# A two-layer kernel behind a retention: the state sums become one scan per unit, weight splits keep out of a block's last two steps, and three casts and splits of the second layer move

## The chip, the cores and the metric

One core of a Trainium2 chip runs the kernel. PE is TensorE (PEld its weight loads), DVE VectorE, ACT ScalarE, POOL GpSimd, SP the engine that issues the DMAs. Every engine takes its own instructions in the order in which the program gives them, and waits where data is missing. The time of a run is device microseconds from start to end of the program; the span of a profile is from the first to the last instruction.

## The reference

```python
def _attn_ref(q, k, v):                    # (4, 8, 576, 64) each
    scores = scale * np.matmul(q, k.transpose(0, 1, 3, 2))
    gamma = 1.0 - 2.0 ** (-5.0 - np.arange(H))
    Dmat = np.where(rel >= 0, gamma[:, None, None] ** rel[None, :, :], 0.0)   # rel = i - j
    return np.matmul(scores * Dmat[None], v)
def _moe_ref(x, w_in, w_out):              # x (2304, 512), w_in (512, 2048), w_out (2048, 512)
    h = x @ w_in
    return (h * (1.0 / (1.0 + np.exp(-1.702 * h)))) @ w_out
def _moe2_ref(x, w_in, w_out, g_ln):       # w_in (512, 1024), w_out (1024, 512)
    h = x @ w_in
    e = np.exp(h - h.max(-1, keepdims=True))
    solu = h * (e / (e.sum(-1, keepdims=True) + 1e-9))
    ln = (solu - mean(solu)) / np.sqrt(var(solu) + 1e-6) * g_ln
    return ln @ w_out
def reference(...):                        # heads side by side make x; then the two layers
    return _moe2_ref(_moe_ref(attn(q, k, v).transpose(0, 1, 3, 2)...))
```

The weights are float64 in memory; everything is computed to about float32.

## The kernel before, in words

**The retention (0 to about 81 us of the profile).** 16 units, one for each pair of heads of one batch, all 128 partitions (64 rows a head). A unit's 576 positions are four chunks of 128 and one of 64. Within a chunk scores are masked by a triangle; what earlier chunks give is carried in a state of 64x64 for each head. PE makes the scores (`st2`, L326), the four chunk states (`states`, L290) and the outputs (`st4`: L347 from the masked scores, L359 and L365 from the states, which are its stationary operand). ACT scales v (`st0`, L278) and copies the states to SBUF (L296). DVE masks (L330), sums the states over the chunks (`st1`, L306: three instructions, each of which needs the one ahead of it) and writes the outputs to `xb` (L377, L382). On DVE and ACT the sequence of a unit is: masks, a piece of weight conversion, outputs of the unit before, state sums. Units are loaded by SP, five buffers in a ring; the constants in two loads.

**The first layer (to about 495 us)** goes over generations `GENS` of the 16 weight slices: slices 0 to 3, 4 to 7, 8 to 15. In each the 2304 tokens go by in six blocks of 384. A step is one slice of one block: `emit_h` (12 matmuls, L417, then the sigmoid L421 on ACT and L422, L426, L427 on DVE) and, one step later, `emit_y` (12 matmuls, L444). Every operand is two numbers, a rounded high part and a low part, and a product is three matmuls: high by high, low by high (of the weight), high by low (of the token tile). The high parts are casts on ACT (L226 of a weight, L398 of a token tile `xs`), the low parts subtractions on POOL (L231, two halves of a weight; L399). `split_x` makes the four token tiles of the next block: tiles 0 and 1 in the block's last step but one, 2 and 3 in its last.

**The background queue** `self.bg` is a list of small pieces: three DVE instructions for each half weight turn float64 words into float32 (`convert`, L203, L206, L209), then come the cast and the two subtractions of `split_weight`, and loads. `background(n)` takes n pieces with a DVE cost and all free ones behind them; `run` calls it at fixed places of each unit and step. So the order on each engine is set by where these calls stand and by what is at the head of the list then. In the first eight slices the two subtractions of a weight are put between the conversions of the next one; the converted weight stands in one of three buffers `T_START`.

**The second layer (to the end)** takes pairs of token tiles; its first product is seven block products instead of eight (`emit_h2`, L520, with weight combinations t1 to t4, b11, b21, b22 and token combinations s1 to s4, a11, a12, a22 from `split_y`; L484 to L489 are sums on DVE). `norm` has three steps: maximum and Exp; product, statistics and a power on POOL (L566); scale (L568). `turn` transposes (L579), `emit_out` makes the second product (L606) with weights w16 to w19. Of these w16 is split along with t3 in the first layer's last block, the casts of w17 to w19 stand at its end, and their subtractions behind the first pair's maximum.

Of the kernel before, what the change touches and what calls it, by code (L numbers as in the profile page):

```python
# [23 lines left out]
P = 128  # L24
# [21 lines left out]
for _name, _w in (  # L46
    ("half", 1), ("g_ln", FB), ("vdec", NP * 3), ("step", NP), ("tri2", LAST), ("tri", CH), ("qdec", NP * CH),
    ("space", 48),
):
    _CC[_name] = (_n, _n + _w)  # L50
    _n += _w
CCONST = _n


def constants():

    gamma = (1.0 - 2.0 ** (-5.0 - np.arange(H))).astype(np.float64)
    c = np.zeros((P, CCONST), np.float64)

    def put(name, a):  # L60
        lo, hi = _CC[name]
        c[:, lo:hi] = a.reshape(P, hi - lo)

    head_of_row = np.arange(P) // D
    qdec = np.zeros((P, NP, CH))
    step = np.zeros((P, NP))
    vdec = np.zeros((P, NP, 3))
    j = np.arange(P)
    for p in range(NP):
        g = gamma[2 * p + head_of_row]  # L70
        qdec[:, p] = g[:, None] ** j[None, :]
        step[:, p] = g ** CH
        for a in range(2):
            vdec[:, p, a] = gamma[2 * p + a] ** -j
        vdec[:, p, 2] = g ** -(j % D)
    put("qdec", qdec)
    put("step", step)
    put("vdec", vdec / math.sqrt(D))
    put("tri", (j[:, None] <= np.arange(CH)[None, :]).astype(np.float64))
    put("tri2", (j[:, None] % D <= np.arange(LAST)[None, :]).astype(np.float64))  # L80
    put("half", np.full((P, 1), -0.5))
    return c.astype(np.float32)
# [54 lines left out]
class Build:  # L137
# [39 lines left out]

    def const(self, name):
        lo, hi = _CC[name]
        return self.at(_M["c"] + lo, hi - lo)  # L180
# [56 lines left out]
    def background(self, n):  # L237

        while self.bg and (n > 0 or not self.bg[0][0]):
            dve, piece = self.bg.pop(0)  # L240
# [4 lines left out]
    def un(self, u):  # L245

        t = self.at(IN_AT[u % NU], CATT)
        st = self.at(ST_AT + (u % 2) * NCH * D, NCH * D).rearrange("r (c e) -> r c e", c=NCH)
# [52 lines left out]
    def st1(self, u):  # L301

        st = self.un(u)[1]
        g = self.const("step")[:, u % NP:u % NP + 1]
        for c in range(1, NCH):
            self.nc.vector.scalar_tensor_tensor(st[:, c], st[:, c - 1], g, st[:, c], ALU.mult, ALU.add)  # L306
# [308 lines left out]
    def run(self):  # L615
# [33 lines left out]
        others = []  # L649
        for f in range(FH):  # L650
            t = T_START[f % 3]
# [3 lines left out]
            for n, p in enumerate(pieces):  # L655
                self.bg.append((1, p))
                if others and n in (0, 4):
                    self.bg.append((0, others.pop(0)))
            hi, *others = self.split_weight(f, t)
            self.bg.append((0, hi))  # L660
        self.bg += [(0, p) for p in others]
# [40 lines left out]
        for g, j, f in steps:  # L702
# [7 lines left out]
            if g == 1 and j == 0 and fl == 1:  # L710

                for i in range(4):
                    first, *rest = self.split_weight(FH + i, T_LATER[i])
                    self.bg += [(1, first)] + [(0, p) for p in rest]
# [9 lines left out]
            bg = 1  # L724
            if fl:
                self.background(bg)
# [3 lines left out]
            if prev is not None:  # L730
                self.emit_y(*prev)
                pg, pj, pf = prev
                if pj == NB - 1:
# [3 lines left out]
                    elif pg == 2:  # L737
# [4 lines left out]
                        if b == "t3":  # L742
                            held += self.split_weight(NF, T_LATER[4], (self.ysp, 2))
# [3 lines left out]
            self.background(1 + (0 if fl else bg))  # L747
# [21 lines left out]
        def out(t):  # L769
# [3 lines left out]
        last = [self.split_weight(NF + i, T_LATER[4 + i], pool) for i, pool in (  # L773
            (1, (self.ysp, 2)), (2, None), (3, (self.zsp, 1))
        )]
        for p in last:
            p[0]()
        y1 = self.split_y(1)
        for piece in y1[:3]:
            piece()  # L780
# [7 lines left out]
        self.emit_h2(0, {"p3": lambda: run(y1[3:])})  # L788
        self.norm(0, 1)
        self.norm(1, 1)  # L790
        for p in last:
            run(p[1:])
# [7 lines left out]
        self.emit_h2(1, {"u2": lambda: self.norm(0, 2, 3), "p3": start})  # L800
# [104 lines left out]
```

## Time and profile before

| | |
|---|---|
| median of 3 runs | 712.52 us (709.82 to 713.21) |
| the profiled execution | 712.1 us, of which the span is 710.3 us |
| PE busy | 685.2 us (96%) |
| DVE busy | 513.4 us (72%) |
| ACT, POOL busy | 231.3 us, 222.8 us |

Matmuls are pipelined and their ends are modelled, so 96% does not mean PE at its peak; how far it is bound has to be read stretch by stretch. A name such as h<-xs,w tells output and inputs of an instruction.

### The profile page before, as it was taken

The numbers are of one execution on the slowest core, as the hardware profiler recorded it, in microseconds if no ns is written. First come the engines' busy times: TensorE is split into PE (matmuls) and PEld (weight loads), VectorE is DVE, ScalarE is ACT, GpSimd is POOL, SyncE is SP. The second block draws the span as 40 slices with busy tenths as digits, with TensorE's granted clock in tenths as the row PEclk, the third lists the DMA queues.
The fourth block names the chain that finished last, engine by engine and source line by source line (L and its number), as shares of the span: only waits on it lengthen the run. The fifth ranks groups of instructions, "written<-read, shape, count | busy, mean of one in ns | idle before, by whom it ended". The sixth has DMA issues, their size and how long they took to land.

```text
span 710.3 us, 11291 instructions
## 1 busy us (share of the span) xinstructions
PE 685.2 (96%) x4454; PEld 632.1 (89%) x4454; DVE 513.4 (72%) x900; ACT 231.3 (33%) x495; POOL 222.8 (31%) x235
## 2 busy tenths in 40 slices
PE   8998989899999899999999999999988999999998
PEld 7777879899999899999999999998666788888887
DVE  3799868777788655636676767768778878877780
ACT  3544243233322322311112121236433435442431
POOL 0211254332332731811111130249932233321300
PEclk9999999999999999999999999999999999999999
DMA  8989500022222100000222110000000000000001
GB/s 327 416 297 343 213 0 1 21 71 88 91 79 71 59 1 1 0 1 28 79 75 88 60 60 30 1 1 4 2 15 1 30 30 31 16 15 30 30 30 45
DMA packets 13301, 49.40 MB, mean 70 GB/s; under 512 B 1472, under 2 KB 2112, under 8 KB 11840
## 3 DMA queue, kind: packets, MB, share of 16 engines
q1 hardware_dynamic: 13248, 48.68, 19.1%
q8 instruction: 35, 0.57, 0.3%
q14 instruction: 18, 0.15, 0.1%
HBM read 43.95 MB, written 4.72 MB: 69 GB/s over the span
## 4 chain that ended last, share of the span: by engine, by line
PE 69%; DVE 14%; issue 7%; POOL 3%; ACT 3%; DMA 2%; SPq 0%; POOLq 0%; DVEq 0%; ACTq 0%
PE yp L444 24%; PE h L417 22%; PE o L606 12%; PE h L520 9%; DMA mem<-in_att 2%; DVE mem L306 2%; POOL xs L399 2%; DVE mem L330 2%; PE zT L579 2%; DVE mem L209 1%; DVE xb L377 1%; DVE mem L559 1%; DVE mem L563 1%; POOL w L231 1%; DVE wraw L206 1%
## 5 line engine op out<-in xcount | busy, mean ns | idle before, releaser
L417 PE MATMUL h<-xs,w 128*128 128x384 f32 x1152 | 219.6, 338 | 6.5 <-POOL xs L399 5.5
L444 PE MATMUL yp<-gs,w 128*128 128x384 f32 x1152 | 220.4, 341 | 0.4 <-DVE gs L426 0.3
L417 PEld LDWEIGHTS h<-xs,w 128*128 128x128 f32 x1152 | 202.0, 188 | 10.1 <-POOL xs L399 8.7
L444 PEld LDWEIGHTS yp<-gs,w 128*128 128x128 f32 x1152 | 204.9, 191 | 2.4 <-DVE gs L426 0.9
L399 POOL TENSOR_TENSOR xs<-xb,xs 128x384 fp32r<-128x384 f32 (+1 forms) x96 | 87.4, 935 | 253.5 <-ACT xs L398 253.4
L421 ACT ACTIVATE mem<-h 128x384 f32<-128x384 f32 x96 | 47.4, 494 | 271.9 <-PE h L417 271.9
L422 DVE TENSOR_TENSOR mem<-h,mem 128x384 f32<-128x384 f32 x96 | 53.6, 558 | 101.3 <-ACT mem L421 100.9
L606 PE MATMUL o<-w,zs 128*128 128x512 f32 (+1 forms) x456 | 104.5, 385 | 0.0
L606 PEld LDWEIGHTS o<-w,zs 128*128 128x128 f32 x456 | 81.3, 188 | 16.8
L427 DVE TENSOR_TENSOR gs<-mem,gs 128x384 fp32r<-128x384 f32 x96 | 75.2, 784 | 11.2 <-ACT gs L424 2.3
L231 POOL TENSOR_TENSOR w<-mem,w 128x512 fp32r<-128x512 f32 x40 | 54.5, 1386 | 76.2 <-ACT w L226 76.2
L426 DVE CAST gs<-mem 128x384 fp32r<-128x384 f32 x92 | 50.0, 544 | 9.5 <-PE yp L444 0.9
L481 POOL TENSOR_TENSOR ys_s<-mem,ys_s 128x256 fp32r<-128x256 f32 x36 | 33.1, 928 | 57.3 <-ACT ys_s L480 57.3
L520 PE MATMUL h<-wt,ys_s 128*128 128x512 f32 x162 | 42.0, 393 | 1.4 <-DVE mem L526 0.7
L526 DVE TENSOR_TENSOR mem<-h,mem 128x512 f32<-128x512 f32 x36 | 24.6, 689 | 22.6 <-PE h L520 12.4
L520 PEld LDWEIGHTS h<-wt,ys_s 128*128 128x128 f32 x162 | 30.2, 188 | 9.1 <-DVE mem L526 1.5
L398 ACT CAST xs<-xb 128x384 fp32r<-128x384 f32 (+1 forms) x96 | 35.4, 430 | 0.0
L566 POOL TENSOR_TENSOR mem<-mem 128x1 f32<-128x1 f32 x18 | 10.0, 557 | 67.1 <-DVE mem L565 63.4
L589 DVE TENSOR_TENSOR zs<-zT,zs 128x512 fp32r<-128x512 f32 x36 | 23.1, 684 | 10.2 <-ACT zs L588 10.2
L226 ACT CAST w<-mem 128x1024 fp32r<-128x1024 f32 x20 | 20.6, 1047 | 27.5 <-DVE mem L209 23.7
L520 PE MATMUL h<-wb,ys_a 128*128 128x512 f32 x108 | 27.9, 393 | 1.7 <-ACT mem L529 1.7
L559 DVE TENSOR_TENSOR mem<-mem 128x1024 f32<-128x1024 f32 x18 | 24.3, 1352 | 3.9 <-ACT mem L557 3.9
(77 smaller groups left out, 725.5 us busy)
## 6 DMA issues: line engine op xcount, KB each, us to landing
mem<-in_att SPq DMA_DIRECT2D x11, 1120.0 KB, 7.8
wraw<-in_w SPq DMA_DIRECT2D x16, 512.0 KB, 11.4
mem<-in_w SPq DMA_DIRECT2D x16, 512.0 KB, 3.8
out<-mem SPq DMA_DIRECT2D x17, 256.0 KB, 2.0
mem<-in_w2in SPq DMA_DIRECT2D x8, 512.0 KB, 3.7
mem<-in_w2out SPq DMA_DIRECT2D x8, 512.0 KB, 3.8
mem<-in_att SPq DMA_DIRECT2D x5, 544.0 KB, 8.4
mem<-in_att SPq DMA_DIRECT2D x4, 576.0 KB, 9.9
```

What stands on the lines that cost most here:

```text
L231: nc.gpsimd.tensor_tensor(lo[:, c], w[:, c], f32(hi[:, c]), ALU.subtract)
L398: nc.scalar.copy(t[:, 0, done:done + n], x)
L399: nc.gpsimd.tensor_tensor(t[:, 1, done:done + n], x, f32(t[:, 0, done:done + n]), ALU.subtract)
L417: nc.tensor.matmul(h[:, 0:TB], a[:, w], x[:, b], start=(n == 0), stop=(n == 3 * KB - 1))
L421: nc.scalar.activation(g, h[:, 0:TB], AF.Sigmoid, scale=1.702)
L422: nc.vector.tensor_tensor(g, h[:, 0:TB], g, ALU.mult)
L426: nc.vector.tensor_copy(gs[:, 0], g)
L427: lo_engine.tensor_tensor(gs[:, 1], g, f32(gs[:, 0]), ALU.subtract)
L444: nc.tensor.matmul(o, a[:, w], gs[:, b], start=(first and i == 0), stop=(last and i == 2))
L481: nc.gpsimd.tensor_tensor(ys[:, 1], src, f32(ys[:, 0]), ALU.subtract)
L520: nc.tensor.matmul(o, a[:, l, k], m[:, w], start=(start and i == 0), stop=(stop and i == 5), skip_group_check=True,)
L606: nc.tensor.matmul(o[:, 0:n], z[:, a, k], b[:, c:c + n], start=(k == 0 and i == 0), stop=(k == FB - 1 and i == 2),)
```

## The change

1. `st1` is one `tensor_tensor_scan` over 256 elements instead of three instructions over 64: each element is the one ahead of it times a factor, plus itself. For this the state has the chunk as its innermost index, so the copy L296 writes and PE's weight loads of L359 and L365 read every fourth element. The factors are a table of 128x1024 (512 KB; zero where a new row of chunks begins), loaded right behind the second load of constants and kept in what was the third buffer of `T_START`, which has two now.
2. `background` has an argument: in a block's last two steps it stops at a cast or subtraction of a weight. In the first eight slices a weight's two subtractions follow its cast directly.
3. In the second layer w16 is split along with t2 and w17 along with t3; w18's cast stays at the end of the first layer and its subtractions come behind the same maximum; w19's cast and subtractions go into the second pair, behind the first tile's norm. The sums of the second pair's tokens come ahead of w18's cast, the casts of its first two combinations behind the first product's copy. A small Exp stands ahead of the first pair.

```diff
-T_START = [_M["t"] + i * SLICE for i in range(3)]
+T_START = [_M["t"] + i * SLICE for i in range(2)]
+SCAN_AT = _M["t"] + 2 * SLICE
...
+    put("scan", step[:, :, None, None] * np.ones((D, 1)) * (np.arange(NCH) > 0))
...
         self.load(_M["c"] + lo, self.const_in[:, lo:hi])
+        self.load(SCAN_AT, self.const_in[:, CCONST:])
...
-    def background(self, n):
+    def background(self, n, splits=True):
         while self.bg and (n > 0 or not self.bg[0][0]):
-            dve, piece = self.bg.pop(0)
+            if len(self.bg[0]) > 2 and not splits:
+                return
+            dve, piece, *_ = self.bg.pop(0)
...
-        st = self.at(ST_AT + (u % 2) * NCH * D, NCH * D).rearrange("r (c e) -> r c e", c=NCH)
+        st = self.at(ST_AT + (u % 2) * NCH * D, NCH * D).rearrange("r (e c) -> r c e", c=NCH)
...
-        g = self.const("step")[:, u % NP:u % NP + 1]
-        for c in range(1, NCH):
-            self.nc.vector.scalar_tensor_tensor(st[:, c], st[:, c - 1], g, st[:, c], ALU.mult, ALU.add)
+        g = self.at(SCAN_AT + u % NP * D * NCH, D * NCH)
+        st = self.at(ST_AT + (u % 2) * NCH * D, NCH * D)
+        self.nc.vector.tensor_tensor_scan(st, g, st, 0.0, ALU.mult, ALU.add)
...
-            for n, p in enumerate(pieces):
-                self.bg.append((1, p))
-                if others and n in (0, 4):
-                    self.bg.append((0, others.pop(0)))
-            hi, *others = self.split_weight(f, t)
-            self.bg.append((0, hi))
-        self.bg += [(0, p) for p in others]
+            self.bg += [(1, p) for p in pieces]
+            self.bg += [(0, p, "split") for p in self.split_weight(f, t)]
...
-            bg = 1
+            bg, free = 1, not have_next or fl < n - 2
             if fl:
-                self.background(bg)
+                self.background(bg, free)
...
-                        if b == "t3":
-                            held += self.split_weight(NF, T_LATER[4], (self.ysp, 2))
+                        if b in ("t2", "t3"):
+                            i = int(b == "t3")
+                            held += self.split_weight(NF + i, T_LATER[4 + i], (self.ysp, 2))
...
-        for p in last:
-            p[0]()
         y1 = self.split_y(1)
-        for piece in y1[:3]:
-            piece()
+        y1[0]()
+        last[0][0]()
+        nc.scalar.activation(self.at(STAT_AT, 1), self.const("half"), AF.Exp)
...
-        self.emit_h2(0, {"p3": lambda: run(y1[3:])})
+        self.emit_h2(0, {"u2": lambda: run(y1[1:3]), "p3": lambda: run(y1[3:])})
         self.norm(0, 1)
         self.norm(1, 1)
-        for p in last:
-            run(p[1:])
+        run(last[0][1:])
...
-        self.emit_h2(1, {"u2": lambda: self.norm(0, 2, 3), "p3": start})
+        self.emit_h2(1, {"u2": lambda: [self.norm(0, 2, 3), run(last[1])], "p3": start})
```

On POOL in the first generation, before, at the end of block 2 (xs0_3_k is tile k of block 3 of generation 0; a row of L231 is one or two halves of a weight):

```order
L231 TENSOR_TENSOR w6_1332<-mem_60,w6_1332 128x512
L399 TENSOR_TENSOR xs0_3_0_1405<-xb_74,xs0_3_0_1405 128x384
L399 TENSOR_TENSOR xs0_3_1_1408<-xb_74,xs0_3_1_1408 128x384
L231 TENSOR_TENSOR w6_1332<-mem_60,w6_1332 128x512
L231 TENSOR_TENSOR w7_1443<-mem_60,w7_1443 128x512 x2
L399 TENSOR_TENSOR xs0_3_2_1465<-xb_74,xs0_3_2_1465 128x384
L399 TENSOR_TENSOR xs0_3_3_1468<-xb_74,xs0_3_3_1468 128x384
```

and the same place in the changed kernel:

```order
L237 TENSOR_TENSOR w6_1334<-mem_60,w6_1334 128x512 x2
L408 TENSOR_TENSOR xs0_3_0_1374<-xb_74,xs0_3_0_1374 128x384
L408 TENSOR_TENSOR xs0_3_1_1377<-xb_74,xs0_3_1_1377 128x384
L408 TENSOR_TENSOR xs0_3_2_1429<-xb_74,xs0_3_2_1429 128x384
L408 TENSOR_TENSOR xs0_3_3_1432<-xb_74,xs0_3_3_1432 128x384
L237 TENSOR_TENSOR w7_1480<-mem_60,w7_1480 128x512 x2
```

The two halves of w7 went from in front of tiles 2 and 3 of block 3 to behind them. At the end of block 0, where the step loop asks for its weights without the new argument, it is the other way: the second half of w4 stood behind tiles 2 and 3 of block 1 and now stands in front of them.

On POOL in the second generation (xs1_3_k, xs1_4_k: tiles of blocks 3 and 4), before:

```order
L231 TENSOR_TENSOR w8_2358<-mem_60,w8_2358 128x512 x2
L399 TENSOR_TENSOR xs1_3_2_2362<-xb_74,xs1_3_2_2362 128x384
L399 TENSOR_TENSOR xs1_3_3_2365<-xb_74,xs1_3_3_2365 128x384
L231 TENSOR_TENSOR w9_2380<-mem_60,w9_2380 128x512 x2
L231 TENSOR_TENSOR w10_2417<-mem_60,w10_2417 128x512 x2
L231 TENSOR_TENSOR w11_2421<-mem_60,w11_2421 128x512 x2
L399 TENSOR_TENSOR xs1_4_0_2458<-xb_74,xs1_4_0_2458 128x192 x2
```

and now:

```order
L408 TENSOR_TENSOR xs1_3_2_2326<-xb_74,xs1_3_2_2326 128x384
L408 TENSOR_TENSOR xs1_3_3_2329<-xb_74,xs1_3_3_2329 128x384
L237 TENSOR_TENSOR w8_2378<-mem_60,w8_2378 128x512 x2
L237 TENSOR_TENSOR w9_2382<-mem_60,w9_2382 128x512 x2
L237 TENSOR_TENSOR w10_2403<-mem_60,w10_2403 128x512 x2
L237 TENSOR_TENSOR w11_2423<-mem_60,w11_2423 128x512 x2
L408 TENSOR_TENSOR xs1_4_0_2427<-xb_74,xs1_4_0_2427 128x192 x2
```

w8 went behind the tiles of block 3, so that eight halves stand in a row ahead of the tiles of block 4. The casts of w8 and w9 stand on ACT behind the sigmoid of block 3's first step, those of w10 and w11 behind that of its second.

On POOL ahead of the second layer (ys0 are the token combinations of the first pair), before:

```order
L231 TENSOR_TENSOR wt2_4314<-mem_60,wt2_4314 128x512 x2
L481 TENSOR_TENSOR ys0_s2_4322<-mem_60,ys0_s2_4322 128x256
L231 TENSOR_TENSOR wb21_4354<-mem_60,wb21_4354 128x512 x2
L481 TENSOR_TENSOR ys0_a11_4360<-mem_60,ys0_a11_4360 128x256
L481 TENSOR_TENSOR ys0_s1_4363<-mem_60,ys0_s1_4363 128x256
L231 TENSOR_TENSOR wt3_4395<-mem_60,wt3_4395 128x512 x2
L231 TENSOR_TENSOR w16_4399<-mem_60,w16_4399 128x512 x2
```

and now:

```order
L237 TENSOR_TENSOR wt2_4283<-mem_60,wt2_4283 128x512 x2
L237 TENSOR_TENSOR w16_4287<-mem_60,w16_4287 128x512 x2
L490 TENSOR_TENSOR ys0_s2_4295<-mem_60,ys0_s2_4295 128x256
L237 TENSOR_TENSOR wb21_4327<-mem_60,wb21_4327 128x512 x2
L490 TENSOR_TENSOR ys0_a11_4333<-mem_60,ys0_a11_4333 128x256
L490 TENSOR_TENSOR ys0_s1_4336<-mem_60,ys0_s1_4336 128x256
L237 TENSOR_TENSOR wt3_4368<-mem_60,wt3_4368 128x512 x2
L237 TENSOR_TENSOR w17_4372<-mem_60,w17_4372 128x512 x2
```

w16 moved up by three token combinations and two weights, and w17 took its place.

## Rows read from the trace of the kernel before

**Rows 1.** Waits of PE over the span: us in total, times, longest

```profile
PE h L417 <- POOL xs L399: 5.5, 6, 1.9
PE o L359 <- DVE mem L306: 4.5, 7, 0.8
```

**Rows 2.** Windows: us, busy of PE PEld DVE ACT POOL, PEclk, DMA, GB/s

```profile
0.00:36.00 36.00, 31.95 (x468) 26.89 (x468) 21.19 (x51) 15.52 (x35) 4.92 (x9) 1.00 0.96 373
36.00:60.00 24.00, 21.20 (x390) 18.55 (x388) 22.95 (x53) 11.04 (x28) 4.34 (x4) 1.00 0.82 302
134.00:138.00 4.00, 2.74 (x9) 2.42 (x10) 3.11 (x4) 0.49 (x1) 2.00 (x2) 0.69 0.00 0
```

**Rows 3.** Timeline of the retention: start us, us, engine, what, [idle before]

```profile
41.41 0.69 DVE L206 SCALAR_TENSOR_TENSOR wraw<-wraw,mem 128x512 uint32<-128x512 uint32 x1
...
44.67 0.93 DVE L306 SCALAR_TENSOR_TENSOR mem<-mem 128x64 f32<-128x64 f32 x3
...
46.38 1.16 PE L326 MATMUL s<-mem 64*128 64x128 f32 x16
...
50.12 1.16 PE L326 MATMUL s<-mem 64*128 64x128 f32 x16
...
52.39 2.48 POOL L231 TENSOR_TENSOR w<-mem,w 128x512 fp32r<-128x512 f32 x2 [14.53 <-ACT w L226]
...
52.72 2.56 DVE L306 SCALAR_TENSOR_TENSOR mem<-mem 128x64 f32<-128x64 f32 x3 [0.63 <-ACT mem L296]
...
55.92 0.38 PE L326 MATMUL s<-mem 64*128 64x128 f32 x2
```

**Rows 4.** Timeline of the second layer, a DVE sum of 256 elements

```profile
546.07 0.42 DVE L489 TENSOR_TENSOR mem<-mem 128x256 f32<-128x256 f32 x1
```

**Rows 5.** Groups by form, PE's weight loads, 0 to 100 us: busy, mean ns

```profile
L326 PEld LDWEIGHTS s<-mem 64*128 64x128 f32 x256 | 15.6, 188 | 1.9 <-DMA mem<-in_att 0.8 <-issue 0.2
L359 PEld LDWEIGHTS o<-mem 64*64 64x64 f32 x192 | 9.8, 132 | 8.7 <-DVE mem L306 6.4 <-ACT mem L296 0.7 <-issue 0.2
```

**Rows 6.** Timeline, starts of blocks 1 and 3 of the first generation

```profile
95.84 3.00 POOL L399 TENSOR_TENSOR xs<-xb,xs 128x192 fp32r<-128x192 f32 x4 [0.50 <-ACT xs L398]
...
129.45 2.24 PE L444 MATMUL yp<-gs,w 128*128 128x384 f32 x12
...
130.94 2.64 POOL L231 TENSOR_TENSOR w<-mem,w 128x512 fp32r<-128x512 f32 x2 [4.97 <-ACT w L226]
...
131.53 1.55 PE L417 MATMUL h<-xs,w 128*128 128x384 f32 x8
...
139.75 2.28 PE L417 MATMUL h<-xs,w 128*128 128x384 f32 x12
```

**Rows 7.** Timeline, start of block 3 of the second generation

```profile
236.31 1.55 PE L417 MATMUL h<-xs,w 128*128 128x384 f32 x8
...
240.65 7.94 POOL L231 TENSOR_TENSOR w<-mem,w 128x512 fp32r<-128x512 f32 x6
...
244.53 2.41 PE L417 MATMUL h<-xs,w 128*128 128x384 f32 x12
...
248.54 2.69 POOL L399 TENSOR_TENSOR xs<-xb,xs 128x192 fp32r<-128x192 f32 x4
```

**Rows 8.** The page's groups, ACT: count, busy us, mean ns, idle before

```profile
L421 ACT ACTIVATE mem<-h 128x384 f32<-128x384 f32 x96 | 47.4, 494 | 271.9 <-PE h L417 271.9
...
L226 ACT CAST w<-mem 128x1024 fp32r<-128x1024 f32 x20 | 20.6, 1047 | 27.5 <-DVE mem L209 23.7
```

**Rows 9.** Timeline, end of the first layer and first pair of the second

```profile
486.07 2.52 PE L444 MATMUL yp<-gs,w 128*128 128x384 f32 x12 [0.35 <-DVE gs L426]
...
500.38 1.67 PE L520 MATMUL h<-wb,ys_a 128*128 128x512 f32 x6 [0.96 <-ACT mem L529]
...
501.31 0.68 DVE L526 TENSOR_TENSOR mem<-h,mem 128x512 f32<-128x512 f32 x1
```

**Rows 10.** Timeline, the first tile's scale behind the power on POOL

```profile
515.81 0.81 DVE L568 TENSOR_SCALAR mem<-mem 128x1024 f32<-128x1024 f32 x1 [0.67 <-POOL mem L566]
```

More of the change, by code (lines that the diff above doesn't have):

```diff
@@ L47 @@
     ("half", 1), ("g_ln", FB), ("vdec", NP * 3), ("step", NP), ("tri2", LAST), ("tri", CH), ("qdec", NP * CH),
-    ("space", 48),
+    ("space", 48), ("scan", NP * D * NCH),
 ):
@@ L51 @@
     _n += _w
-CCONST = _n
+CCONST, _n_consts = _CC["scan"][0], _n
 def constants():
     gamma = (1.0 - 2.0 ** (-5.0 - np.arange(H))).astype(np.float64)
-    c = np.zeros((P, CCONST), np.float64)
+    c = np.zeros((P, _n_consts), np.float64)
     def put(name, a):
@@ L107 @@
 R2_AT = R1_AT + 4 * NCH * CH
-T_START = [_M["t"] + i * SLICE for i in range(3)]
+T_START = [_M["t"] + i * SLICE for i in range(2)]
+SCAN_AT = _M["t"] + 2 * SLICE
 RAW_AT = [_M["att"], _M["att"] + SLICE]
-T_LATER = T_START + [_M["att"] + (2 + i) * SLICE for i in range(5)]
+T_LATER = T_START + [SCAN_AT] + [_M["att"] + (2 + i) * SLICE for i in range(5)]
 U_AT = [T_LATER[i] for i in range(4)]
@@ L647, in run @@
                 load_w()
-        others = []
         for f in range(FH):
-            t = T_START[f % 3]
+            t = T_START[f % 2]
             pieces = []
@@ L713, in run @@
                     first, *rest = self.split_weight(FH + i, T_LATER[i])
-                    self.bg += [(1, first)] + [(0, p) for p in rest]
+                    self.bg += [(1, first, "split")] + [(0, p, "split") for p in rest]
             if start:
@@ L746, in run @@
                     held.pop(0)()
-            self.background(1 + (0 if fl else bg))
+            self.background(1 + (0 if fl else bg), free)
             if g == len(GENS) - 1 and last_block:
@@ L770, in out @@
             self.emit_out(t, zs.pop(t))
-        last = [self.split_weight(NF + i, T_LATER[4 + i], pool) for i, pool in (
-            (1, (self.ysp, 2)), (2, None), (3, (self.zsp, 1))
-        )]
-        for p in last:
-            p[0]()
+        last = [
+            self.split_weight(NF + i, T_LATER[4 + i], pool) for i, pool in ((2, None), (3, (self.zsp, 1)))
+        ]
         y1 = self.split_y(1)
-        for piece in y1[:3]:
-            piece()
+        y1[0]()
+        last[0][0]()
+        nc.scalar.activation(self.at(STAT_AT, 1), self.const("half"), AF.Exp)
         def run(pieces):
```

## The prediction

> **What bounds the kernel now.** I read the waits of PE first, then windows stage by stage, then timelines of the places where PE waits. In the waits two lines belong to this change: PE's h matmuls wait for POOL's token tiles (5.5 us), and the retention's L359 for the state sums L306 (4.5 us) [rows 1]. The windows tell three regimes apart [rows 2]. From 0 to 36 us the DMA engines are 0.96 busy at 373 GB/s, so what is loaded early shifts what follows. From 36 to 60 us DVE is busy 22.95 of 24 us: it bounds the retention. [...]
>
> **The sum** is made against the profiled execution's own 712.1 us (span 710.3, 1.8 around it), 0.4 under the median of 712.52. About 0.5% (3.6 us) is what a measurement of this kernel can tell from no change.
>
> **The scan.** Three instructions take 0.93 us where POOL is quiet [rows 3]. No scan is in this trace. From below it is bounded by a DVE sum of 256 elements from two SBUF inputs, 0.42 us [rows 4]; from above by the three it replaces, since each of its elements also needs the one before. I take 0.69 us, near the middle, the duration of an instruction on 512 elements from two SBUF inputs [rows 3], as if each element took two turns. In quiet units that saves 0.24 (0 to 0.51). Every fourth unit POOL subtracts a weight at the same time: there L306 takes 2.56 us, because two of its three instructions each wait for a half of POOL's 2.48 [rows 3]. The scan waits once: POOL's first half ends at 52.39 + 1.24 = 53.63, the scan then lasts to about 54.3 instead of 55.28, which saves 1.0 (0.75 if the scan is no faster than the three, 1.25 at 0.42). From the third unit on, where DMA stops being the bound, there are nine quiet units and three of the other sort on DVE's chain: 9 x 0.24 + 3 x 1.0 = 5.2. PE allows that much: a unit takes it 3.74 us undisturbed (46.38 to 50.12) and 5.80 with the wait (50.12 to 55.92), so three times 2.06 and some more at the start are idle time that can go [rows 3].
>
> [...]
>
> The table adds 512 KB ahead of the second unit's v: 0.52 MB / 373 GB/s = 1.4 us later [rows 2], in full, since DMA bounds that stretch (0 if its stream has gaps of that size, which a share of 0.96 does not leave). Later loads keep ahead: the 302 GB/s of 36 to 60 us rise by a tenth, still under 373. Retention: -5.2 + 1.4 = -3.8.
>
> PE now reads its state weights at every fourth element, and ACT writes them so; no row shows either. From below 0 (a load runs beside the matmul before it). From above I take twice the streaming part of a load: 128 columns take 188 ns and 64 take 132 [rows 5], so 64 columns stream in 56 ns, and 16 such loads a unit could add 0.9 us. I take 0, the value of loads that stay hidden.
>
> **No splits in the last two steps.** Three block starts change.
> Block 3 of the first generation: w7 (130.94, 2.64 us) stands on POOL ahead of tiles 2 and 3. The first step of the block takes 139.75 - 131.53 = 8.22 us instead of 2 x 2.08 = 4.16 (129.45 to 131.53 is one half step) [rows 6]. With w7 behind the tiles the 4.06 go; PE's waits for POOL's tiles are only six in the whole span [rows 1], so blocks without a split there start without the loss. -4.1 (-3.5 to -4.3).
> Block 3 of the second generation: the same, 244.53 - 236.31 = 8.22 [rows 7], so 4.06 go. But now eight halves stand ahead of block 4's tiles. Counted from block 3's start: sigmoid from 2.1 to 2.6, cast to 3.65 [rows 8], eight halves at 7.94 / 6 = 1.32 to 14.3, eight tile pieces at 2.69 / 4 = 0.67 to 19.7 [rows 7]. PE starts block 4 at 4 x 4.16 = 16.64 and wants the last tile's low part at its twelfth matmul, 18.5. A new wait of about 1.2 us (1.7 if a tile piece takes 0.75, [rows 6]), which costs 1.2 if the clock holds and some twice that, up to 3.4, if it falls as in the old one (where waits of about 2 us cost 4.06). I take 2.0: net -2.1 (-2.9 to -0.7).
> Block 1 of the first generation: here w4's second half now goes ahead of tiles 2 and 3. POOL idled 0.50 before them [rows 6]; 1.24 - 0.50 = +0.8 (0.7 to 1.5, if the clock stays low longer).
> Two buffers instead of three for converted weights cost nothing: a buffer is written again one whole weight later, over 10 us.
>
> **The second layer.** w16 and w17 come on POOL ahead of work that DVE runs beside. DVE's casts and sums there wait for a POOL piece as L306 did, up to 1.24 each, and PE already waits 0.35 for such a cast at 486.07 [rows 9]. I count +1.0 (-0.4, if that wait goes, to +2.5, two pieces). The earlier copy behind the first product removes a wait of 0.96 at 500.38, but the product behind the next needs a DVE addition that runs from 501.31 to 501.99 behind the second pair's sums [rows 9], whose place on DVE is the same: nothing gained. If those sums got faster, the 0.96 would come. The early Exp hides behind PE's products in both versions. w19's subtractions now follow the first tile's power on POOL with no wait between; the scale on DVE starts at 515.81 just behind that power [rows 10] and PE's transposes wait for it. Whoever is second waits: 0 to +1.24, I take +0.5. Together +1.5.
>
> Sum: -3.8 - 4.1 - 2.1 + 0.8 + 1.5 = -7.7, so 712.1 - 7.7 = 704.4 us.
>
> **Rivals.**
> The scan is as cheap as a plain sum (0.42): quiet units save 0.51 and the three others 1.25, 8.3 in all, but PE's undisturbed 3.74 us a unit becomes the bound and leaves the 3 x 2.06 = 6.2 of these rows. Then 703.4. For it: PE's idle time is there; against it: each element depends on the last.
> The scan saves nothing in quiet units: 3 x 0.75 = 2.3 remain, and 707.3.
> The splits only move the wait: block 4 of the second generation loses 3.4 and DVE behind a crowded POOL 2.5 + 1.2 more in the second layer. That is -3.8 - 4.1 - 0.7 + 0.8 + 3.7 = -4.1: 708.0, the end of what can be told from no change. For it: the eight halves in a row; against it: the new wait of 1.2 us is little more than half of the one after which the clock fell.
> PE's strided weight loads bound the retention. By the upper value above a unit takes 3.74 + 0.9 = 4.64 us; in twelve units before, three of 5.80 and nine of 3.74 give 4.26 on average, so the retention loses 12 x 0.38 = 4.6 instead of gaining 5.2, and the time is 714.2. [...] Against it: L359 loads at 132 ns run beside matmuls, with room. It decides for slower (over 716.1) from 0.16 us a unit more, 1.06 or 66 ns a load, just above the 56 of my bound; a load that streams at a quarter of the pace (168 ns more) would give 12 x (6.43 - 4.26) = 26 us and 736.
> The change does what it says by the order of instructions, so I keep no rival for that.
>
> **How the numbers follow.** Forecast 0.55, cheap scan 0.12, no saving in quiet units 0.08, moved waits 0.13, strided loads 0.12 (half of it near 714, half of it milder or worse). Faster by over 0.5% of the median is under 709.0: the first three nearly whole and 0.6 of the fourth, 0.8; less what errs in all cases alike (the two buffers, DMA later on), 0.74. Slower, above 716.1: 0.07 from loads above 66 ns. The rest, 0.19, is the same. The likeliest case by itself spans 700.5 to 707.5 (its terms' bounds by chance on one side or the other). The range reaches to both scan cases and the moved waits: 699.0 to 710.0.
>
> **What would show it.** The scan's duration in quiet units (0.69) and beside POOL (about 1.5), and PE's unit at 3.74 with no jump of 2; a weight load of L359 near 132 ns (188 would mean the strided rival); the second unit's v later by 1.4; no wait at block 3 in both generations and the clock at 1.00 there; a wait at block 4 of the second generation, with its clock; a longer start of block 1; DVE casts around 480 to 490 us stretched by POOL, and the scale L568 at 0.81 or at about 2. The prediction is wrong if the retention does not end about 4 us earlier, or if first steps of 8 us only turn up in other blocks.

## The result and the profile after

Timed side by side, the changed kernel takes 704.96 us (median of 5, 703.06 to 706.28) against 712.52 (709.82 to 713.33): 0.9906 of the time before, 95% interval 0.9886 to 0.9925. The forecast was 704.4 us, range 699.0 to 710.0. The profiled execution takes 704.96 us, its span is 703.2, 7.1 less than before. In the changed file most lines moved: L306 is now L315, L359 is L368, L326 is L335, L296 is L305, L231 is L237, L399 is L408, L417 is L426, L444 is L453, L520 is L529, L568 is L577, L579 is L588.

Waits of PE after (us in total, times, longest), the first three:

```profile
PE zT L588 <- DVE mem L577: 3.5, 2, 1.8
PE h L426 <- POOL xs L408: 2.8, 4, 1.8
PE o L368 <- DVE mem L315: 2.3, 3, 1.1
```

The two waits that the change aims at are halved (5.5 and 4.5 before, [rows 1]); the one on top is in the second layer and was 2.7. The milestones of both timelines give the account. A step is counted from the start of its first h product to that of the next one; a half step is its twelve h products or its twelve y products. The last row starts at the last h products but one of the first layer (483.48 before, 475.38 after).

| stretch | forecast | before | after | difference |
|---|---|---|---|---|
| start to the first h product | -3.8 | 76.68 | 73.67 | -3.0 |
| block 1, first step | +0.8 | 8.47 | 10.39 | +1.9 |
| block 3, first step, first generation | -4.1 | 8.22 | 4.25 | -4.0 |
| block 3, first step, second generation | -4.1 | 8.22 | 4.16 | -4.1 |
| block 4, first step, second generation | +2.0 | 4.24 | 5.51 | +1.3 |
| end of the first layer to the first transposes | +1.5 | 33.20 | 34.15 | +0.95 |

These sum to -6.95; what is left of the 7.1 lies within what the pace of the half steps, told below, can make (23 slow ones in place of 30, an estimated 0.28). The sum is right, and so are the signs of all rows, but two of them need an account of their own: the retention comes near by other means than forecast, and block 1 lost more than the bound.

**Retention.** Timeline of after: start, duration, engine, what, in brackets the idle time before and what ended it.

```profile
26.96 0.68 DVE L315 TENSOR_TENSOR_SCAN mem<-mem 128x256 f32<-128x256 f32 x1
...
45.92 1.16 PE L335 MATMUL s<-mem 64*128 64x128 f32 x16
...
49.84 1.16 PE L335 MATMUL s<-mem 64*128 64x128 f32 x16
...
50.71 2.89 POOL L237 TENSOR_TENSOR w<-mem,w 128x512 fp32r<-128x512 f32 x2 [12.95 <-ACT w L232]
...
51.30 1.23 DVE L315 TENSOR_TENSOR_SCAN mem<-mem 128x256 f32<-128x256 f32 x1 [0.80 <-ACT mem L305]
...
53.92 1.16 PE L335 MATMUL s<-mem 64*128 64x128 f32 x16
```

The scan lasts 0.68 us where POOL is quiet, as taken (0.69), and 1.23 beside POOL; there it ends 51.30 + 1.23 - 50.71 = 1.82 us after POOL began, forecast 1.93. It ends as if it waited for the end of POOL's first piece, 1.27 after that one's start: 0.55 behind it. In the trace of before the first two of the three sums take 1.02 and 1.19 there, each ending 0.09 after one of POOL's two pieces (1.26 each), and the third takes 0.29 behind both. POOL's two pieces take 2.89 (1.27 and 1.66) in place of 2.48 [rows 3]. What holds one engine back beside the other is not shown. The unit beside POOL takes PE 53.92 - 49.84 = 4.08 us in place of 5.80. But a quiet unit takes 49.84 - 45.92 = 3.92, more than the 3.74 of before [rows 3]. PE never waits in it, and it did not before either, as the window of that unit of before shows (us, busy of PE, PEld, DVE, ACT, POOL, PEclk, DMA, GB/s):

```profile
46.38:50.12 3.74, 3.74 (x77) 3.48 (x73) 3.67 (x11) 0.64 (x2) 0.00 (x0) 1.00 0.91 308
```

The reason for the 0.18 stands in PE's weight loads (groups by form of after; count, busy us, mean ns); ACT's write is longer too:

```profile
L368 PEld LDWEIGHTS o<-mem 64*64 64x64 f32 x192 | 12.7, 204 | 4.2 <-DVE mem L315 3.4 <-issue 0.2
...
L305 ACT ACTIVATE mem<-T,mem 128x256 f32<-128x256 f32 x9 | 6.6, 736 | 7.2 <-PE T L299 7.2
```

A load of a state at every fourth element takes 204 ns in place of 132 [rows 5], ACT's write 736 ns in place of 468. The loads run beside each other: 192 of 132 ns would be 25.3 us in a row and kept PEld busy for 9.8, 192 of 204 would be 39.2 and kept it busy for 12.7. In a quiet unit all loads together keep PEld busy for 3.67 us in place of 3.48, and that is the size of the 0.18. From the seventh unit's scores to the first h product (31.83 to 76.68 before, 32.95 to 73.67 after) the account closes: the three units beside POOL give 1.94, 1.72 and 1.74, seven quiet ones take 0.18 each, -5.40 + 1.27 = -4.13, and the stretch is 44.85 before and 40.72 after. The start before it is 1.1 late.

**Block 1** of the first generation, POOL and PE of after:

```profile
91.08 2.51 POOL L237 TENSOR_TENSOR w<-mem,w 128x512 fp32r<-128x512 f32 x2 [2.91 <-ACT w L232]
...
93.55 3.46 POOL L408 TENSOR_TENSOR xs<-xb,xs 128x192 fp32r<-128x192 f32 x4
...
95.51 1.33 PE L426 MATMUL h<-xs,w 128*128 128x384 f32 x3 [1.80 <-POOL xs L408]
...
97.55 4.04 PE L453 MATMUL yp<-gs,w 128*128 128x384 f32 x12
...
101.39 2.56 PE L426 MATMUL h<-xs,w 128*128 128x384 f32 x12
```

Both halves of w4 now stand ahead of the tile pieces. PE's waits in the step grow from 2.13 to 2.88 us, by the 0.75 that was forecast (1.24 - 0.50). Most of the rest is clock: after these waits twelve y products take 3.84 us (97.55 to 101.39), 3.03 before (granted clock 0.66 on average) and 2.08 undisturbed. In this window of after (columns as above) the granted clock is 0.50 over all 3.89 us.

```profile
97.50:101.39 3.89, 3.89 (x14) 3.89 (x13) 2.51 (x5) 1.45 (x4) 0.00 (x0) 0.50 0.00 0
```

**Blocks 3 and 4.** Starts of block 3 in both generations, and block 4 of the second:

```profile
131.34 2.28 PE L426 MATMUL h<-xs,w 128*128 128x384 f32 x12
...
135.59 2.28 PE L426 MATMUL h<-xs,w 128*128 128x384 f32 x12
...
231.62 2.24 PE L426 MATMUL h<-xs,w 128*128 128x384 f32 x12
...
235.78 2.24 PE L426 MATMUL h<-xs,w 128*128 128x384 f32 x12
...
248.50 1.55 PE L426 MATMUL h<-xs,w 128*128 128x384 f32 x8
250.54 0.79 PE L426 MATMUL h<-xs,w 128*128 128x384 f32 x3 [0.49 <-POOL xs L408]
251.65 0.45 PE L426 MATMUL h<-xs,w 128*128 128x384 f32 x1 [0.31 <-POOL xs L408]
251.93 2.25 PE L453 MATMUL yp<-gs,w 128*128 128x384 f32 x12
```

The old waits are gone [rows 6, 7]. The new one at block 4 is there (0.49 + 0.31 us of idle time; by the starts the h products take 251.93 - 248.50 = 3.43 us in place of 2.08), the products behind it keep their pace of 2.08 (granted clock 1.00 from 248.50 to 252.74), and the step is 1.27 longer, about the 1.2 of the case in which the clock holds.

**Second layer:**

```profile
478.60 2.35 PE L453 MATMUL yp<-gs,w 128*128 128x384 f32 x12 [0.98 <-DVE gs L435]
...
494.10 1.67 PE L529 MATMUL h<-wt,ys_s 128*128 128x512 f32 x6 [0.70 <-DVE mem L535]
...
507.66 2.94 POOL L237 TENSOR_TENSOR w<-mem,w 128x512 fp32r<-128x512 f32 x2
...
507.73 1.74 DVE L577 TENSOR_SCALAR mem<-mem 128x1024 f32<-128x1024 f32 x1 [0.67 <-POOL mem L575]
...
509.53 1.09 PE L588 MATMUL zT<-mem 128*128 128x128 f32 x8 [1.82 <-DVE mem L577]
```

PE waits longer for a cast beside the two added splits (0.98; 0.35 in [rows 9]) and a second time behind it (0.43 at 486.25), less inside the first pair (0.70 for 0.96), and longer for the first scale, which takes 1.74 us beside w19's subtractions in place of 0.81 [rows 10].

### The profile page after: what moved, and what is told of

Read it like the earlier page. It is cut to its first block, busy times and chain, and to the rows that moved or that the text cites. A ratio compares the mean times of both kernels' runs of the same rounds, so it can differ in the third digit from the quotient of the medians.

```text
span 703.2 us, 11252 instructions
## 1 busy us (share of the span) xinstructions
PE 682.4 (97%) x4454; PEld 634.8 (90%) x4454; DVE 511.1 (73%) x868; ACT 235.1 (33%) x496; POOL 224.7 (32%) x235
## 4 chain that ended last, share of the span: by engine, by line
PE 76%; DVE 11%; ACT 4%; issue 3%; DMA 2%; POOL 2%; SPq 0%; DVEq 0%; POOLq 0%; ACTq 0%
PE yp L453 26%; PE h L426 26%; PE o L615 12%; PE h L529 8%; DMA mem<-in_att 2%; PE zT L588 2%; POOL xs L408 1%; PE o L368 1%; DVE mem L493 1%; DVE mem L315 1%; ACT w L232 1%; DVE mem L568 1%; DVE mem L572 1%; DVE mem L339 1%; PE s L335 1%
## 5 line engine op out<-in xcount | busy, mean ns | idle before, releaser
L426 PE MATMUL h<-xs,w 128*128 128x384 f32 x1152 | 218.7, 338 | 3.8 <-POOL xs L408 2.8
L453 PE MATMUL yp<-gs,w 128*128 128x384 f32 x1152 | 218.5, 339 | 1.4 <-DVE gs L435 1.0
L426 PEld LDWEIGHTS h<-xs,w 128*128 128x128 f32 x1152 | 202.2, 188 | 6.2 <-POOL xs L408 4.7
L453 PEld LDWEIGHTS yp<-gs,w 128*128 128x128 f32 x1152 | 202.7, 189 | 3.4 <-DVE gs L435 1.3
L408 POOL TENSOR_TENSOR xs<-xb,xs 128x384 fp32r<-128x384 f32 (+1 forms) x96 | 88.6, 948 | 243.5 <-ACT xs L407 243.5
L436 DVE TENSOR_TENSOR gs<-mem,gs 128x384 fp32r<-128x384 f32 x96 | 77.8, 810 | 11.2 <-ACT gs L433 2.3
L237 POOL TENSOR_TENSOR w<-mem,w 128x512 fp32r<-128x512 f32 x40 | 55.0, 1400 | 75.8 <-ACT w L232 75.8
L435 DVE CAST gs<-mem 128x384 fp32r<-128x384 f32 x92 | 52.5, 570 | 9.1 <-PE yp L453 0.5
L529 PE MATMUL h<-wt,ys_s 128*128 128x512 f32 x162 | 42.0, 393 | 2.2 <-DVE mem L535 1.4
L529 PEld LDWEIGHTS h<-wt,ys_s 128*128 128x128 f32 x162 | 30.2, 188 | 9.9 <-DVE mem L535 2.2
L529 PE MATMUL h<-wb,ys_a 128*128 128x512 f32 x108 | 27.7, 392 | 0.7 <-ACT mem L538 0.7
L568 DVE TENSOR_TENSOR mem<-mem 128x1024 f32<-128x1024 f32 x18 | 24.2, 1345 | 4.0 <-ACT mem L566 4.0
```

Source lines behind the costliest of these rows:

```text
L237: nc.gpsimd.tensor_tensor(lo[:, c], w[:, c], f32(hi[:, c]), ALU.subtract)
L408: nc.gpsimd.tensor_tensor(t[:, 1, done:done + n], x, f32(t[:, 0, done:done + n]), ALU.subtract)
L426: nc.tensor.matmul(h[:, 0:TB], a[:, w], x[:, b], start=(n == 0), stop=(n == 3 * KB - 1))
L435: nc.vector.tensor_copy(gs[:, 0], g)
L436: lo_engine.tensor_tensor(gs[:, 1], g, f32(gs[:, 0]), ALU.subtract)
L453: nc.tensor.matmul(o, a[:, w], gs[:, b], start=(first and i == 0), stop=(last and i == 2))
```

## The experiments

Each was timed beside the kernel before; a ratio is to that, with its 95% interval. Each run's kernel has its own line numbers (the h products are L417 to L426, the y products L444 to L454).

**One part of the change at a time.** e1: the kernel before with the scan, its table, the interleaved layout and two buffers.

```diff
-        for c in range(1, NCH):
-            self.nc.vector.scalar_tensor_tensor(st[:, c], st[:, c - 1], g, st[:, c], ALU.mult, ALU.add)
+        self.nc.vector.tensor_tensor_scan(st, g, st, 0.0, ALU.mult, ALU.add)
```

> The kernel before with the scan, its table, the interleaved layout of the states and the two buffers, and nothing else of the change. Theory A (read from the trace of after: PE bounds every unit, 3.92 us, since a state's weight load takes 204 ns in place of 132; the three units beside POOL fall from 5.80 to 4.07; the start is 1.1 late): first h product at 73.7 in place of 76.68 us, total 3.0 less, ratio 0.9958, 709.5 us. Theory B (the terms as forecast: DVE bounds, quiet units 3.74 or less, 3.8 gained): first h product at 72.9, ratio 0.9947, 708.7 us. Rival C (most of the 3.0 belongs to the new order of converts and splits, not to the scan): first h product at 75.5 or later, ratio above 0.998.

Measured 708.09 us, ratio 0.9952 (0.9921 to 0.9984). The first h product starts at 74.60, quiet units take 3.92 (42.92 to 46.84), units beside POOL 4.08 (50.76 to 54.84). Theory A holds for the units; the first h product lies between A and C, because this execution's start was later (its seventh unit's scores at 33.86, 32.95 in the changed kernel). By time alone B could not be told from A. One thing was not expected. Block 1 is as before the change, and PE waits 2.32 us in all (2.13 before the change), but the products behind the waits run at 2.08:

```profile
95.57 0.79 PE L423 MATMUL h<-xs,w 128*128 128x384 f32 x3 [0.92 <-POOL xs L405]
96.85 0.44 PE L423 MATMUL h<-xs,w 128*128 128x384 f32 x1 [0.49 <-POOL xs L405]
97.13 2.24 PE L450 MATMUL yp<-gs,w 128*128 128x384 f32 x12
99.21 2.24 PE L423 MATMUL h<-xs,w 128*128 128x384 f32 x12
```

Its first step takes 99.21 - 91.92 = 7.29 us, 3.13 more than one without waits (4.16); the same step of the kernel before takes 8.47. So waits of nearly the same length cost over a microsecond more or less; what decides, their length does not say.

e2: the rule on splits and the plain order of converts and splits alone.

```diff
-            self.background(1 + (0 if fl else bg))
+            self.background(1 + (0 if fl else bg), free)
```

> The kernel before with the rule on splits and the plain order of converts and splits, three buffers, no scan. Theory A (the rule alone makes every change of the first layer): first step of block 1 takes 10.4 us and the half steps behind it 2.12, that of block 3 4.2 in both generations, that of block 4 of the second generation 5.5; 5.1 less in all, ratio 0.993, 707.4 us. Rival B (the long start of block 1 comes from the scan, which shifts DVE's converts against POOL): first step of block 1 about 9.2 us as forecast, half steps at 2.08 behind it, 6.9 less in all, ratio 0.990, 705.6 us.

Measured 707.53 us, ratio 0.9925 (0.9900 to 0.9951), as A said, with B's 0.990 at the edge. Block 1's first step, without any scan:

```profile
94.31 1.20 PE L419 MATMUL h<-xs,w 128*128 128x384 f32 x6
...
100.89 4.04 PE L446 MATMUL yp<-gs,w 128*128 128x384 f32 x12
104.73 2.96 PE L419 MATMUL h<-xs,w 128*128 128x384 f32 x12
```

10.42 us, so the long start of block 1 belongs to the rule on splits with its order of converts and splits. The half steps of 2.12 behind it, which A had as its consequence, are not there: they run at 2.08. That part of A fell.

e3: the moved casts and splits of the second layer alone.

```diff
-                        if b == "t3":
+                        if b in ("t2", "t3"):
```

> The kernel before with the moved casts and splits around the second layer alone. Theory A (the trace of after): first product of the second layer 0.7 later, fourth and fifth product without the wait of 0.96, first transposes 0.8 later behind the power on POOL; in all 0.95 more, ratio 1.0013, 713.5 us. Theory B (as forecast): 1.5 more, ratio 1.0021, 714.0 us. Rival C (these moves gain, and the loss near 480 us is the first layer's new timing): ratio below 1.000, 712.0 us or less.

Measured 714.68 us, ratio 1.0012 (0.9982 to 1.0043), which excludes none of the three. The trace does, for one execution of each: from the h product at 484.47 to the first transposes at 519.73 it takes 35.26 us, 2.06 more than before.

```profile
487.67 2.39 PE L444 MATMUL yp<-gs,w 128*128 128x384 f32 x12 [0.95 <-DVE gs L426]
...
494.92 2.67 PE L444 MATMUL yp<-gs,w 128*128 128x384 f32 x12 [0.62 <-DVE gs L426]
...
504.33 1.66 PE L520 MATMUL h<-wt,ys_s 128*128 128x512 f32 x6 [1.25 <-DVE mem L526]
...
519.73 1.09 PE L579 MATMUL zT<-mem 128*128 128x128 f32 x8 [1.82 <-DVE mem L568]
```

The wait of 0.96 in the first pair is replaced by one of 1.25. So rival C is out: these moves lose, 0.95 us in the changed kernel and 2.06 here.

**The layout alone.** e4: the states interleaved, three sums per unit as before.

```diff
-        st = self.at(ST_AT + (u % 2) * NCH * D, NCH * D).rearrange("r (c e) -> r c e", c=NCH)
+        st = self.at(ST_AT + (u % 2) * NCH * D, NCH * D).rearrange("r (e c) -> r c e", c=NCH)
```

> The kernel before with the states' layout interleaved as the scan wants it, but still three sums per unit on DVE: no scan, no table. Theory A (the stride costs PE 0.18 us in every unit): weight loads of the states at 204 ns, ACT's state write at 0.73 us in place of 0.47, quiet units 3.92 us; first h product at 76.68 + 12 x 0.18 = 78.8 us or a little later, ratio 1.003 to 1.005, 715 us. Rival B (the loads stay hidden, and the 0.18 of after belong to the scan's place on DVE): quiet units 3.74, ratio 1.000, 712.5 us. Rival C (strided sums take DVE longer and DVE bounds): quiet units above 4.2, ratio above 1.008, 718 us.

Measured 712.51 us, ratio 0.9999 (0.9970 to 1.0028): the time does not tell A from B. The trace does: the state's load takes 202 ns, the quiet units 3.92, and the first h product starts at 78.39.

```profile
L359 PEld LDWEIGHTS o<-mem 64*64 64x64 f32 x192 | 13.5, 202 | 6.4 <-DVE mem L306 4.1 <-ACT mem L296 1.2 <-issue 0.2
...
43.91 1.16 PE L326 MATMUL s<-mem 64*128 64x128 f32 x16
...
47.83 1.16 PE L326 MATMUL s<-mem 64*128 64x128 f32 x16
...
53.63 2.44 DVE L306 SCALAR_TENSOR_TENSOR mem<-mem 128x64 f32<-128x64 f32 x3 [0.90 <-ACT mem L296]
```

DVE's sums take longer here (1.08 in quiet units) than the scan's 0.68, and the quiet unit of PE is the same 3.92. That settles who bounds it: PE, by its strided loads, and the scan's saving in quiet units buys nothing. Beside POOL three sums still take 2.44, the scan 1.23: there the saving counts.

**The table.** e5: the changed kernel, with the table made on the chip: `g`, filled with ones and zeros at the start, is multiplied by each pair's factor.

```diff
-        self.load(SCAN_AT, self.const_in[:, CCONST:])
+            self.nc.scalar.mul(g, g, self.const("step")[:, p:p + 1])
```

> The changed kernel, but the scan's table is not loaded: eight fills on DVE and four multiplications on ACT make it at the start, so 512 KB less go through the DMA queues ahead of the second unit's v. Theory A (the table's place in a DMA-bound start costs what it weighs): first h product 1.1 to 1.4 earlier than with the table (73.7 to 72.4 us), total 1.2 less, ratio to the kernel before 0.989, 703.8 us. Rival B (the start is not bound by the bytes in front of the second unit, since later loads follow anyway): first h product within 0.4 of 73.7, total as the changed kernel, ratio 0.9906. Rival C (the fills and multiplications come in the way of the first unit on DVE and ACT): later than 74, ratio above 0.992.

Measured 705.08 us, ratio 0.9898 (0.9873 to 0.9923); the first h product starts at 74.20. The interval holds the ratios of A and B both, not C's; the milestone is later than A's and B's. It fits C's (later than 74) without C's cause: the fills and multiplications end at 4.87, ahead of ACT's first use of v at 7.02. And the table's delay is there at the place where the forecast has it, ACT's first use of the second unit's v (timeline, the changed kernel first):

```profile
12.73 1.06 ACT L287 ACTIVATE mem<-mem 128x256 f32<-128x256 f32 x2 [3.42 <-DMA mem<-in_att]
```

```profile
10.46 1.06 ACT L289 ACTIVATE mem<-mem 128x256 f32<-128x256 f32 x2 [2.13 <-DMA mem<-in_att]
```

Counted from the first unit's v, the second follows 4.64 to 4.81 us later in the six kernels with the table loaded and 3.36 to 3.60 without (the kernel before, e2 to e5, and e8 below, which has its table from the chip too; 4.03 in e11). So 512 KB cost about 1.0 to 1.4 us there, for the 1.4 forecast. That e5's first h product is late all the same is clock. The fifth unit's scores start at 24.31 in this execution and at 24.30 in e8's; the sixth's follow 5.52 us later here and 4.25 there. Windows (us, busy of PE, PEld, DVE, ACT, POOL, PEclk, DMA, GB/s), e5 first:

```profile
24.31:27.84 3.53, 3.53 (x35) 3.31 (x34) 3.53 (x8) 1.88 (x5) 0.84 (x1) 0.54 1.00 414
```

```profile
24.30:28.55 4.25, 4.00 (x77) 3.67 (x73) 4.25 (x9) 2.59 (x6) 1.30 (x2) 1.00 1.00 415
```

Without these 1.27 us e5's first h product would start at 72.9 (an estimate), between A's 72.4 and 73.7. How much of the delay is left at the end of the start varies: with the table loaded the seventh unit's scores start between 32.95 and 33.86, in e8 at 32.47, without any table at 31.83 to 32.56. The time does not show it.

**Block 1.** e6: the changed kernel; the one background call that escapes the rule obeys it.

```diff
-                self.background(1)
+                self.background(1, fl < n - 2)
```

> The changed kernel, with the rule on splits kept in the one call that escapes it, the extra background step of the first block: w4 no longer stands on POOL ahead of tiles 2 and 3 of block 1. Theory A (the long start of block 1, 10.39 us, is POOL's 2.51 us for w4 ahead of the tiles, and the clock that fell behind it): only ACT's late cast (0.9) and the tile's own pieces remain, first step 6 us if the clock holds and 8 if it falls, 2.4 to 4.4 less than the changed kernel, ratio 0.985 to 0.987, 701.5 us. Rival B (ACT's cast of the tiles, which stands behind the sigmoid and the copy of the step before, sets the end, and POOL only follows): first step 9 us or more, at most 1.4 less, ratio 0.989 or more.

Measured 699.62 us, ratio 0.9825 (0.9798 to 0.9852), below A's. POOL and PE at the same place:

```profile
91.01 2.42 PE L426 MATMUL h<-xs,w 128*128 128x384 f32 x11
...
91.31 2.38 POOL L408 TENSOR_TENSOR xs<-xb,xs 128x192 fp32r<-128x192 f32 x4 [3.10 <-ACT xs L407]
...
93.74 0.44 PE L426 MATMUL h<-xs,w 128*128 128x384 f32 x1 [0.31 <-POOL xs L408]
...
94.02 2.24 PE L453 MATMUL yp<-gs,w 128*128 128x384 f32 x12
...
96.10 1.20 PE L426 MATMUL h<-xs,w 128*128 128x384 f32 x6
```

The first step takes 5.09 us in place of 10.39. ACT casts these tiles earlier too (90.89, 92.44 in the changed kernel), since w4's cast no longer stands in front of them; rival B is out. How much of the gain is that cast's, and how much the subtractions', is not separated. The later splits move by one place, and the wait at block 4 of the second generation goes as well; 0.26 us of it turn up at block 5.

e7: e6, and the tiles cast ahead of the sigmoid in every block's last step.

```diff
+        then()          # split_x of the next block's tiles 2 and 3
         g = self.at(_M["g"] + (f % 2) * TB, TB)
```

> As the run before (w4 behind the tiles), and in every block's last step ACT casts the next block's tiles 2 and 3 right behind the h products, ahead of the step's sigmoid. Theory A: block 1's first step falls to 4.2 us with no wait of PE in it, 6.2 less than the changed kernel, ratio 0.982, 699 us; nothing else moves (the first step of block 4 of the second generation stays at 5.5). Rival B (the sigmoid, now behind four casts, is late for the y products): each block's last step grows by 0.3 to 1 us, seventeen times, ratio above 0.990.

Measured 700.31 us, ratio 0.9840 (0.9810 to 0.9869). Block 1's first step is 4.24 us (91.55 to 95.79) without a wait, as A has it, but the time is not below e6's. B's cause isn't there either: no step's end is long. What is long is every half step but two from 87 to 257 us, 2.12 in place of 2.08.

e8: e7 and e5 together, and w8 to w11 spread over two blocks.

```diff
-                    self.bg += [(1, first, "split")] + [(0, p, "split") for p in rest]
+                    self.bg += [(1, first, "split"), (1, rest[0], "split"), (0, rest[1], "split")]
```

> The two before together (no table load, w4 behind the tiles, tiles cast first), and the eight halves that stand on POOL ahead of block 4 of the second generation spread over two blocks. Theory A (the costs are separate and add): first h product at 72.5 us, first steps of block 1 and of block 4 of the second generation 4.2 us each, 1.2 + 6.2 + 1.3 = 8.7 less than the changed kernel, ratio 0.978, 697 us. Rival B (spread halves come in the way of another block's tiles or of DVE): a first step above 5 us in block 5 of the second or block 0 of the third generation, ratio 0.981 or more.

Measured 702.27 us, ratio 0.9856 (0.9825 to 0.9886): not faster than e6, and A's 697 missed (its first h product starts at 73.18, A had 72.5). No first step is above 5 us, so B's cause is missing too. Again 79 half steps of the profiled execution take 2.12.

**Without the second layer's moves.** e9: the scan, the rule on splits and e6's line, the second layer as before.

> The kernel before with the scan and its table, and with the rule on splits and w4 behind the tiles of block 1, but the second layer as before. Theory A (the second layer's moves cost 0.7 + 0.8 and gain 0.55): 1.0 less than the changed kernel with w4 behind the tiles (699.6), ratio 0.981, 698.7 us; waits of PE at the end of the first layer 0.35 in place of 0.95 and 0.62, first transposes' wait 1.0 in place of 1.8, fourth product's wait 0.96. Rival B (the moves are worth it once the first layer is short): ratio 0.984 or more, 701 us. On the pace of the half steps (2.08 or 2.12 us) neither theory says anything: up to 3 us either way.

Measured 697.83 us, ratio 0.9796 (0.9764 to 0.9827): the fastest of all, 15 us below the kernel before. PE's waits at this place are as A has them (0.96 for the fourth product, 1.10 at the transposes). Against e6 the intervals overlap; the traces give e6 the waits of e3 again (0.97, 0.61, 1.28, 1.84).

e10: e9 with e8's spread splits.

> As the run before, and w8 to w11 split two by two in blocks 3 and 4 of the second generation. Theory A (the wait at block 4 is eight halves in a row): its first step 4.2 us in place of 5.5, 1.3 less, ratio 0.979, 697.4 us. Rival B (with no wait of PE left from block 1 on, most half steps of the first two generations take 2.12 us as in the two kernels without such waits, about 75 of them in place of the usual 10 to 70): 0.04 x 40 = 1.6 us given back or more, ratio 0.981 or above.

Measured 700.30 us, ratio 0.9818 (0.9787 to 0.9849): no gain over e9. A had nothing left to take, since e9's block 4 no longer waits (one wait of 0.49 at block 5, which e10 moves by one block). B's slow half steps were not there in the profiled execution, only 6.

e11: e9 without the scan.

> The kernel before with the rule on splits and w4 behind the tiles of block 1, three sums per unit as before, no scan, no table, second layer as before. Theory A (the scan's three units beside POOL are worth 3.0 net of the strided loads and the table): 3.0 more than with the scan, ratio 0.985, 701.9 us; first h product at 76.5. Rival B (the splits, unchanged in the retention, take the scan's gain along): ratio 0.982 or less.

Measured 705.43 us, ratio 0.9875 (0.9830 to 0.9919), with single runs from 698.37 to 707.05. The first h product is at 76.75. The time is 3.5 above A, and B is out; but what fills most of the 3.5, as far as one profile of each tells, is the pace. Here 142 half steps of about 175 take 2.12, in e10's profile 6; PE rows of e11 first, then of e10, both with the granted clock at 1.00:

```profile
150.03 2.28 PE L419 MATMUL h<-xs,w 128*128 128x384 f32 x12
152.15 2.28 PE L446 MATMUL yp<-gs,w 128*128 128x384 f32 x12
```

```profile
150.34 2.24 PE L425 MATMUL h<-xs,w 128*128 128x384 f32 x12
152.42 2.24 PE L452 MATMUL yp<-gs,w 128*128 128x384 f32 x12
```

142 x 0.04 = 5.7 us. Taken off, e11's span is 704.1 - 5.7 = 698.4 and e9's (61 such half steps) 698.5 - 2.4 = 696.1: an estimate of 2.3 us for the scan, from one execution of each. The first h products say the same: 74.40 in e9, 76.75 here.

## Why the prediction was right, and where it was not

- **Scan, quiet units: wrong.** No row of before shows a scan; the 0.69 was the author's choice between 0.42 and 0.93, and the scan took 0.68. But the nine quiet units counted on DVE's chain save nothing. DVE was busy 22.95 of 24 us, but PE ran without a gap in those units, at 3.74 us; a busy engine was taken for the bound. The text held its 5.2 against PE's idle time of all units together (6.2), and all of that lies in the three units beside POOL. In place of -2.2 stands 0.18 more per unit (e4).
- **Strided loads: the direction of the rival, at a sixth of its price.** Loads take 72 ns more, above the 66 that the rival named as its threshold, and the kernel is not slower. The step of the rival that failed is that each load was charged to PE in full: 16 x 72 = 1.15 us of loading per unit lengthen the unit by 0.18. That loads overlap stood in the forecast's own row (192 of 132 ns in 9.8 us [rows 5]). Taking 0 was wrong too. ACT's strided write grew as well, 736 ns in place of 468; why a strided access takes longer no run shows.
- **Scan beside POOL: right, and larger.** The scan loses time once (1.23 us in place of 0.68) and ends where forecast (1.82 after POOL's start for 1.93), but it was counted as 1.0 per unit; PE's wait of 2.06 goes nearly whole (1.9), less 0.18 for the loads. That is -5.4 in place of -3.0, which covers the two errors above; the retention came out at -3.0 for -3.8 by compensation, and its sign (an end about 4 us earlier) is met only roughly.
- **Table: right where it was read, not settled behind.** Forecast 1.4; about 1.0 to 1.4 at the second unit's v, 1.1 at the seventh unit's scores of the changed kernel against the kernel before, 0.5 against e8, and nothing that a time shows.
- **Block 3, twice: right** (-4.0, -4.1). e2 shows that the rule alone does it.
- **Block 4 of the second generation: right in kind**, 1.3 for 2.0; the granted clock held at 1.00.
- **Block 1: mis-sized.** The wait grew by 0.75, as worked out, but the step by 1.9, above its bound of 1.5: the matmuls at the lower clock were priced at nothing in the middle value (twelve y products 3.84 at a granted 0.50, in place of 3.03 at 0.66). e6 shows w4 as the cause: without it the step is 5.09.
- **Second layer: right in kind**, 0.95 for 1.5. The wait of 0.96, said to bring nothing, brought 0.55, and the scale beside POOL cost 0.8 for the 0.5 taken; e3 shows how far this depends on what arrives when (2.06).
- The time is right because the errors cancel (-0.5 in the second layer, -0.7 at block 4, +1.1 in block 1, +0.8 in the retention): its central value owes its closeness to that, which is luck.

## What to carry to other kernels

Time saved on an engine that was busy 95% (DVE, 22.95 of 24 us; 0.93 to 0.68 a unit) was worth nothing here, where another one ran without a gap (PE, 3.74 of a quiet unit's 3.74): look at the unit's period and at who has no idle time in it. A layout chosen for one engine was paid by the others that read or write it (PE's loads 132 to 204 ns, ACT's write 468 to 736); price it there, but by what its group's busy time grows (PEld 3.48 to 3.67 us in a quiet unit), not by the mean of one instruction times their number (16 x 72 ns = 1.15 us), since they overlapped. A rule about order must hold in every call that takes from the queue: the one call left out cost 5.3 us in one step, where the whole change gained 7.6.

## What was not expected of the hardware

- Reading 64 weight columns at every fourth float32 takes PE 202 to 204 ns (132 in a row), ACT's write of 256 such elements 734 to 736 ns (468), three DVE sums 1.08 us (0.93).
- Nearly the same waits of PE cost more in one execution than in another. With 2.32 us of waits block 1's first step took 7.29 us in e1, at a granted clock of 1.00; with 2.13 it took 8.47 before, and with 2.35 it took 102.09 - 93.36 = 8.73 in e3, at 0.66 and 0.60 in the twelve y products behind the waits. In the retention the clock fell to 0.54 in e5 and stayed at 1.00 in e8, after 4.3 us in which PE was busy for 2.7 in both. What decides is open.
- Half steps of the first layer take 2.08 or 2.12 us in long stretches, at a granted clock of 1.00 in both: 30 of 2.12 before, 23 after, and 6 to 142 in the eleven experiments, 0.2 to 5.7 us of a run. None of the edits can be shown to set it (7 in e6, 61 in e9, 6 in e10, 142 in e11), and past 300 us it is rare except in e9 and e11. Some changes of pace come behind a half step that is itself longer: in e9 47 half steps of 2.08 end with one of 2.42 at 192.47 us, and 23 of 2.12 follow; before, 2.12 ends behind 2.38 (152.47) and 2.45 (297.65). In the changed kernel 2.12 turns to 2.08 at 150.42 without one. What it comes from is open; it may be a good part of the spread between runs of one kernel, and enough to hide any single term of this account.
